# Moving the loads of gates and places of the experts to another queue and into seven blocks

## Chip, cores and metric

The kernel runs on one core of a Trainium2 chip. The metric is the device time of one launch in microseconds (us); lower is better.

## What is computed

A linear attention feeds a mixture of eight experts. The attention takes q, k and v of 8 batches, 8 heads, 576 rows and 64 columns; its output is seen as 4608 tokens of 512 values. Every token is routed to its two best experts.

```python
def _attn_ref(q, k, v):
    phi = lambda x: np.where(x > 0, x, np.exp(x) - 1.0) + 1.0
    q_p, k_p = phi(q), phi(k)
    kv = np.einsum('bhsd,bhse->bhde', k_p, v)
    num = np.einsum('bhsd,bhde->bhse', q_p, kv)
    den = np.einsum('bhsd,bhd->bhs', q_p, np.sum(k_p, axis=2))[..., None] + 1e-06
    return num / den

    # experts, x is 4608 x 512, w1 is 8 x 512 x 1024, w2 is 8 x 1024 x 512
    noisy_logits = x @ w_gate + np.log1p(np.exp(x @ w_noise)) * noise
    top2 = np.argpartition(-noisy_logits, 2, axis=1)[:, :2]
    # top2_w: the two gates of a token, a softmax over its two logits
    for e in range(E):
        for k in range(2):
            mask = top2[:, k] == e
            h = np.maximum(x[mask] @ w1[e], 0.0)
            out[mask] += top2_w[mask, k, None] * (h @ w2[e])
```

## The kernel before

The first part of the kernel computes attention and routing, and it scatters every token's row twice into a table in DRAM, `x_sorted` (`dispatch`, line 396, GpSimd): once into the list of first visits ("F") of the lower numbered of its two experts, once into the list of second visits ("S") of the other. A row of this table is 1152 bytes: the 512 values, and behind them four words, which are the token's number, its two gates, and its place in the list of first visits. A tile is 128 rows of such a list.

The second part works the experts through, block by block; a block is up to four tiles of one expert. `mm1` (line 652) makes the hidden layer of a block in eight pieces, and ScalarE takes each out of PSUM with a Relu (line 654). `mm2` (line 667) makes the output of one tile. VectorE multiplies it with the gate (lines 671 to 675), and where the tile is one of second visits, it adds the first visits' results `L`. `put` stores first visits into the DRAM table `part` by SyncE's queue (line 683) and scatters second visits to the output by GpSimd (line 689). `gather` (line 635, GpSimd) fetches `L` for the next block from `part`. It may start only when all first visits of the experts of lower number are stored. Tiles called "M" hold the end of both lists of an expert and are fetched by `mid_gather` (line 505, GpSimd); they count as both. GpSimd puts a MEMSET as a gap behind each of its indirect DMAs.

The order on every engine is the order of the program. `interval` (line 699) weaves the `mm1` of block i with the `mm2` and the `put` of block i-1, and ends with the `gather` for block i+1. In the main loop there are 20 blocks: block 0 is the last of expert 0 (called c0, tiles F6 to F9, the last a half tile), 1 and 2 belong to expert 1, 3 and 4 to expert 2, 5 to 7 to expert 3, and so on to 17 to 19 of expert 7. Each half of the weights of the experts 4 to 7 is loaded by GpSimd's queue (line 443) at the start of one of the blocks 1, 3, 4, 6, 8, 9, 11 and 12.

The gates and places of the lists are brought to SBUF by `meta_load` (line 450), as 16 bytes out of each row. For the first tiles of the experts 0 to 3 this is done early, in rounds, by SyncE's queue. The rest goes by GpSimd's queue: `prepare(0)`, called in `routing`, makes one load, and `prepare(1)` to `prepare(7)`, called all together in block 0, make 13, two for each of the experts 1 to 6 (F and S) and one of ten tiles for expert 7. In the queue of GpSimd they stand behind the last dispatch and ahead of two `mid_gather`s and of the first weights of expert 4. `metas(e)`, called in the last block before expert e, makes indices out of the lists on VectorE: `meta_s` out of the loaded list (lines 464 to 467) and `mid_meta` out of the M rows (lines 518 to 522). On VectorE they stand ahead of the outputs of the block before.

Of the kernel before, what the change touches and what calls it, by code (L numbers as in the profile page):

```python
# [15 lines left out]
P = 128  # L16
# [3 lines left out]
E = 8  # L20
# [392 lines left out]
class PhaseB:  # L413
# [31 lines left out]
    def meta_load(self, e, kind, i0, nt, group=None):  # L445

        m = self.mp.tile([P, nt, 4], INT32, name=f"meta{e}{kind}{i0}", bufs=1)
        row = self.row(e, kind, i0)
        rows = self.x_sorted[row : row + nt * P, HD // 2 : HD // 2 + 4]
        r = (self.nc.gpsimd if group is None else self.nc.sync).dma_start(out=m[:], in_=rows.rearrange("(t p) c -> p t c", p=P))  # L450
        self.early(r, kind, group)
        for i in range(nt):
            self.m[e, kind, i0 + i] = {"gate": m[:, i, 1 : 2] if kind == "F" else m[:, i, 2 : 3]}
        if kind == "S":
            self.raw[e] = m
# [456 lines left out]
def routing(pa, pb, c, a0, a1, a2):  # L912

    b0, b1 = pb.block(0, ("F", 4, 2)), pb.block(1, ("F", 3, 2))
    b2 = pb.block(2, ("F", 2, 2))
    a3, c0 = pb.block(3, ("F", 0, 3)), pb.block(0, ("F", 6, 4))
    pb.w_tiles(2, 1)
    pb.w_load(2, 0)
    pa.dispatch(2, 5, 6)
    pb.w_load(2, 1)  # L920
    pa.dispatch(2, 6, 9)
    pb.w_tiles(3, 1)
    pb.meta_load(0, "F", 4, 2, 2)
    pb.x_load(b0, 2)
    pb.meta_load(1, "F", 3, 2, 2)
    pb.x_load(b1, 2)
    pa.rt_b(3)
    pa.rt_c(3)
    pb.mm2(a0, 0)
    pb.put(a0, 0)  # L930
    pa.dispatch(3, 0, 6, (0,))
    pb.w_load(3, 0)
    pb.mm2(a0, 1)
    pb.put(a0, 1)
    pa.rt_a(4)
    pb.mm1(a1, *range(6))
    pa.rt_b(4)
    pb.mm1(a1, 6, 7)
    pa.rt_c(4)
    pa.dispatch(4, visits=(0,))  # L940
    pb.w_load(3, 1)
    pa.dispatch(3, 0, 6, (1,))
    pa.dispatch(4, visits=(1,))
    pb.mids()
    pb.meta_load(2, "F", 2, 2, 2)
    pb.x_load(b2, 2, False)
    pb.meta_load(3, "F", 0, 3, 2)
    pb.x_load(a3, 2, False)
    pb.interval(a2, a1, (), b0)
    pb.interval(b0, a2, (), b1)  # L950
    pb.prepare(0)
    pb.x_load(c0, turned=False)
    pb.interval(b1, b0, (), b2)
    pb.interval(b2, b1, (), a3)
    pb.interval(a3, b2, (), c0)
    return a3, c0
# [14 lines left out]

WEIGHTS = [(1, 3), (4, 6), (8, 9), (11, 12)]
TURNED = 3
AT = 0


@with_exitstack
def kernel(
    ctx: ExitStack,
    tc: tile.TileContext,  # L980
    q: bass.AP,
    k: bass.AP,
    v: bass.AP,
    moe_w_gate: bass.AP,
    moe_w_noise: bass.AP,
    moe_noise: bass.AP,
    moe_w1: bass.AP,
    moe_w2: bass.AP,
    out: bass.AP,
):  # L990
    nc = tc.nc
    x_sorted = nc.dram_tensor("x_sorted", (NO_X + 2 * P, ROW_W // 2), INT32, kind="Internal").ap()
    part = nc.dram_tensor("part", (NO_P + 2 * P, HD), FP32, kind="Internal").ap()
    nc.scalar.preload_act_table_set(ACT_SET)

    consts = ctx.enter_context(tc.tile_pool(name="consts", bufs=1))
    zrow = consts.tile([P, ROW_W // 2], INT32, name="zrow")
    pb = PhaseB(ctx, tc, moe_w1, moe_w2, x_sorted, part, out)
    pb.cp = consts
    ps = lambda cx, name, bufs, side: cx.enter_context(tc.tile_pool(name=name, bufs=bufs, space=PSUM, side=side))  # L1000
    ps_b = ps(ctx, "ps_b", 2, "left")
    pb.ps_h = pb.ps_y = [ps_b]
    with ExitStack() as order:
        order.enter_context(tc.manual_schedule())
        right = lambda name, bufs: ctx.enter_context(tc.tile_pool(name=name, bufs=bufs, side="right"))
        with ExitStack() as rout:
            ps_misc = ps(rout, "ps_misc", 2, "left")
            with ExitStack() as attn:
                psa = [ps(attn, "ps_num", 1, "right"), [(ps_misc, "misc"), (ps_b, "b")]]
                pa = PhaseA(attn, rout, tc, q, k, v, x_sorted, psa)  # L1010
                for t in "kqv":
                    pa.load(0, t)
                c = pa.c = pb.c = build_constants(tc, consts, moe_w_gate, moe_w_noise, moe_noise)
                pa.buffers()
                for t in "kv":
                    pa.load(1, t)
                first = attention(pa, pb, c, x_sorted, zrow)
            pb.ps_h = [ps(ctx, "ps_h2", 3, "right")]
            pb.ps_t = ps(ctx, "ps_t", 1, "right")
            pb.xps += [pb.xp] * 3 + [right("B_x2", 1)]  # L1020
            pb.np = right("B_n", 3)
            pb.lp = right("B_l", 8)
            pb.yp += [right("B_y2", 6)] * 2
            pb.wp.append(right("B_w2", 3))
            prev, cur = routing(pa, pb, c, *first)
        pb.ps_y.append(ps(ctx, "ps_y2", 2, "left"))
        pb.wp.append(ctx.enter_context(tc.tile_pool(name="B_w3", bufs=1, side="left")))
        pb.late = ctx.enter_context(tc.tile_pool(name="B_late", bufs=1, side="left"))
        blocks = [cur] + [pb.block(e, *parts) for e in range(1, E) for parts in PLAN[e]]

        todo = {}
        for e, at in zip(range(4, E), WEIGHTS):
            for k, i in enumerate(at):
                todo.setdefault(i, []).append((e, k))
        for i, b in enumerate(blocks):
            pb.left += [b["e"]] * sum(kind != "S" for kind, _ in b["tiles"])
        for i, b in enumerate(blocks):
            if i == AT:
                for e in range(1, E):
                    pb.prepare(e)  # L1040
            nxt = blocks[i + 1] if i + 1 < len(blocks) else None
            for nb in blocks[i + 1 : i + 4] if i == 0 else blocks[i + 3 : i + 4]:
                pb.x_load(nb, turned=nb["e"] >= TURNED)
            if (i == 0 or b["e"] != blocks[i - 1]["e"]) and b["e"] + 1 < E - 1:
                pb.mid_gather(b["e"] + 1)
            if nxt and nxt["e"] != b["e"]:
                pb.metas(nxt["e"])

            parts = todo.get(i, [])
            for e2, k in parts:  # L1050
                if k == 0:
                    pb.w_tiles(e2, {4: 1, 5: 2}.get(e2, 0))
            pb.interval(b, prev, parts, nxt)
            prev = b
        pb.interval(None, prev)
    pb.general()
# [30 lines left out]
```

## Time and profile before

| | us |
|---|---|
| median of three runs | 424.74 |
| lowest and highest | 424.2 and 425.75 |
| the profiled execution | 428.73 |
| its span | 426.9 |

In the profile, PE is TensorE, PEld its weight loads, DVE VectorE, ACT ScalarE, POOL GpSimd and SP SyncE. Over the span PE is busy 82%, POOL 68%, DVE 43% and ACT 41%. Each such share mixes the two parts of the kernel; the rows further down are of the second part, and they have the time in us from the start of the span. A row of a timeline has the start, the duration, the engine, the line, the operation, what is written from what, and in brackets how long the engine sat idle before and what ended that. Durations of DMA instructions are those of the issue; when the data has landed shows in who waits for it.

### The profile page before, as it was taken

Reading aid. Unit: us, or ns where it says so; the run is one execution under the profiler, and the core shown is the slowest. Engines: PE = TensorE matmul, PEld = TensorE weight load, DVE = VectorE, ACT = ScalarE, POOL = GpSimd, SP = SyncE. Lnnn points to the kernel's source line nnn. Section 1 sums busy time; section 2 is a strip of 40 time slices with the busy share of each in tenths; the row PEclk is TensorE's granted clock in tenths of the full one; section 3 lists DMA queues with packets and bytes.
Section 4 is the critical chain, followed back from the end, with each engine's and each line's share of the span. In section 5 each row is a group of like instructions: output and inputs, shape, how many; then the busy total and the mean of one; then the engine's idle time right before and its main releaser. Section 6 shows DMA issues by size and latency. Waiting matters only on the chain.

```text
span 426.9 us, 6907 instructions
## 1 busy us (share of the span) xinstructions
PE 348.1 (82%) x2517; PEld 206.5 (48%) x2517; DVE 184.2 (43%) x474; ACT 173.4 (41%) x310; POOL 289.3 (68%) x422
## 2 busy tenths in 40 slices
PE   3863577453757888999999999999999999999930
PEld 1363466353545454655556556545545544554410
DVE  2837989995777741111342305223322222412220
ACT  1738654760442432455445434443343343344200
POOL 7120229886888878737707675878848868989880
PEclk9987655688698998999999999999999999999985
DMA  9999999498998999994496999999998999944440
GB/s 128 205 208 208 236 208 229 105 227 198 214 191 204 204 219 227 254 364 105 87 252 191 171 189 250 211 245 253 187 284 174 226 280 232 212 157 154 140 165 25
DMA packets 77025, 85.58 MB, mean 200 GB/s; under 512 B 36415, under 2 KB 59730, under 8 KB 76982
## 3 DMA queue, kind: packets, MB, share of 16 engines
q0 software_dynamic: 36624, 64.02, 70.1%
q1 hardware_dynamic: 38694, 20.86, 21.9%
q10 hardware_dynamic: 1664, 0.18, 0.5%
q8 instruction: 21, 0.34, 0.3%
q14 instruction: 22, 0.18, 0.1%
HBM read 77.13 MB, written 33.79 MB: 260 GB/s over the span
## 4 chain that ended last, share of the span: by engine, by line
PE 41%; POOL 25%; DMA 18%; DVE 6%; issue 5%; ACT 2%; POOLq 0%; DVEq 0%; ACTq 0%
PE b L652 20%; PE b L667 19%; DMA w<-in_moe_w_dram 6%; POOL x_sorted L396 6%; POOL L L635 5%; POOL out_dram L689 5%; DMA kq<-in_q_dram 5%; DMA L<-part,mgi 2%; POOL gap L642 2%; POOL gap L697 2%; DMA xt<-x_sorted 2%; POOL gap L387 1%; DMA part<-y 1%; POOL kq L161 1%; PE t L599 1%
## 5 line engine op out<-in xcount | busy, mean ns | idle before, releaser
L654 ACT ACTIVATE hT<-b 128x256 bf16<-128x256 f32 (+5 forms) x224 | 101.7, 461 | 151.1 <-PE b L652 148.1
L652 PE MATMUL b<-xt,w 128*128 128x256 bf16 (+5 forms) x896 | 149.1, 314 | 15.4 <-DMA xt<-x_sorted 13.4
L667 PE MATMUL b<-w,hT 128*128 128x512 bf16 (+1 forms) x640 | 146.1, 384 | 0.0
L652 PEld LDWEIGHTS <-w 128*128 128x128 bf16 x896 | 86.5, 99 | 70.8 <-issue 20.3
L396 POOL DMA_INDIRECT x_sorted<-xr,posi x72 | 75.0, 1041 | 32.3 <-DMA w<-in_moe_w_dram 12.5
L667 PEld LDWEIGHTS <-hT 128*128 128x128 bf16 (+1 forms) x640 | 59.5, 100 | 64.6 <-issue 5.0
L176 ACT ACTIVATE e<-kq 128x2304 bf16<-128x2304 bf16 x16 | 33.2, 2120 | 24.8 <-PE misc L207 10.3
L635 POOL DMA_INDIRECT L<-part,gi x34 | 34.9, 1026 | 6.1 <-issue 6.1
L689 POOL DMA_INDIRECT out_dram<-y,si x34 | 33.7, 992 | 6.1 <-issue 5.3
L635 POOL DMA_INDIRECT L<-part,mgi x12 | 12.0, 1001 | 32.0 <-DMA xt<-x_sorted 15.4
L207 PE MATMUL b<-v,e 64*128 64x192 bf16 x144 | 19.3, 309 | 11.2 <-DVE e L188 8.7
L671 DVE SCALAR_TENSOR_TENSOR y<-b,mgate,L 128x512 f32<-128x512 f32 (+1 forms) x12 | 8.9, 745 | 42.7 <-DMA L<-part,mgi 24.6
L270 PE MATMUL num<-kvbd,pqt 128*64 128x162 bf16 x288 | 18.3, 299 | 11.0 <-DVE lwt L288 10.1
L281 DVE TENSOR_TENSOR xr<-num,rden 128x768 bf16<-128x768 f32 x24 | 21.9, 953 | 4.8 <-DMA x_sorted<-xr,posi 4.5
L207 PEld LDWEIGHTS <-e 64*128 64x128 bf16 x288 | 17.0, 122 | 14.2 <-DVE e L188 9.4
L270 PEld LDWEIGHTS <-pqt 128*64 128x64 bf16 x288 | 15.3, 146 | 13.6 <-DVE lwt L288 8.1
L188 DVE TENSOR_TENSOR e<-e,kq 128x2304 bf16<-128x2304 bf16 x16 | 21.5, 1358 | 0.3
L642 POOL MEMSET gap<- 128x416 f32 x46 | 21.2, 460 | 0.1
L697 POOL MEMSET gap<- 128x416 f32 x45 | 21.0, 466 | 0.0
L207 PE MATMUL misc<-v,e 64*128 64x192 bf16 x144 | 19.5, 309 | 0.6 <-DMA v<-in_v_dram 0.6
L387 POOL MEMSET gap<- 128x192 f32 x72 | 19.8, 275 | 0.0
L256 ACT COPY pqt<-misc 128x1024 bf16<-128x1024 bf16 (+1 forms) x15 | 13.6, 905 | 14.9 <-PE misc L254 14.7
(184 smaller groups left out, 327.8 us busy)
## 6 DMA issues: line engine op xcount, KB each, us to landing
w<-in_moe_w_dram POOLq DMA_DIRECT2D x16, 1024.0 KB
part<-y SPq DMA_DIRECT2D x39, 256.0 KB, 5.5
kq<-in_k_dram POOLq DMA_DIRECT2D x8, 576.0 KB
kq<-in_q_dram POOLq DMA_DIRECT2D x8, 576.0 KB
v<-in_v_dram POOLq DMA_DIRECT2D x8, 576.0 KB
x_sorted<-xr,posi POOLq DMA_INDIRECT x72
xn<-x_sorted SPq DMA_DIRECT2D x4, 256.0 KB, 6.8
part<-y SPq DMA_DIRECT2D x7, 128.0 KB, 6.9
```

The source lines that it names most:

```text
L176: self.nc.scalar.activation(out=e, in_=x, func=ACT.Exp)
L207: nc.tensor.matmul(out=self.kvps[g, h, j][:, KVM * i : KVM * i + KVM], lhsT=e[half, hp, ci, :], rhs=v[half, hp::4, 64 * ci : 64 * ci + 64] ...
L270: nc.tensor.matmul(out=ps[half, hp, KVW * i : KVW * i + KVW], lhsT=self.pqt[g, 3 * t + i][:, hp, half], rhs=self.kvbd[g][:, j, hp, :], sta ...
L387: self.nc.gpsimd.memset(self.c["gap"], 0.0)
L396: r = self.nc.gpsimd.indirect_dma_start(out=self.x_sorted, out_offset=bass.IndirectOffsetOnAxis(ap=self.r["posi", u][:, ci - c0, sl : sl + ...
L635: r = nc.gpsimd.indirect_dma_start(out=L[0:m].bitcast(INT32), out_offset=None, in_=self.part.bitcast(INT32), in_offset=bass.IndirectOffset ...
L642: nc.gpsimd.memset(self.c["gap2"][:], 0.0)
L652: nc.tensor.matmul(out=ps[:, 0:n], lhsT=w1[:, dc, fc * P : fc * P + P], rhs=b["xt"][:, dc, 0:n], start=(dc == 0), stop=(dc == 3))
L654: nc.scalar.activation(out=b["hT"][:, fc, 0:n], in_=ps[:, 0:n], func=ACT.Relu)
L667: nc.tensor.matmul(out=ps[i * m : i * m + m], lhsT=b["hT"][:, f, t * P : t * P + m], rhs=w2[:, f, :], start=(fc == 0), stop=(fc == 8 // n ...
L689: r = nc.gpsimd.indirect_dma_start(out=self.out, out_offset=bass.IndirectOffsetOnAxis(ap=self.m[e, kind, i]["si"][0:m], axis=0), in_=y[0:m ...
L697: nc.gpsimd.memset(self.c["gap2"][:], 0.0)
```

## The change

The 13 loads of the experts 1 to 7 go by ScalarE's queue instead of GpSimd's, and those of expert e are issued at the start of block e-1, so in the blocks 0 to 6. The test on `e` also sends the remaining load of expert 0 by SyncE's queue.

```diff
@@ meta_load
-        r = (self.nc.gpsimd if group is None else self.nc.sync).dma_start(out=m[:], in_=rows.rearrange("(t p) c -> p t c", p=P))
+        r = (self.nc.scalar if e and group is None else self.nc.sync).dma_start(out=m[:], in_=rows.rearrange("(t p) c -> p t c", p=P))
@@
-AT = 0
@@ main loop
         for i, b in enumerate(blocks):
-            if i == AT:
-                for e in range(1, E):
-                    pb.prepare(e)
+            if i < E - 1:
+                pb.prepare(i + 1)
```

## Rows read from the trace of the kernel before

**Rows 1.** The page's chain that ended last: shares of the span by engine.

```profile
PE 41%; POOL 25%; DMA 18%; DVE 6%; issue 5%; ACT 2%; POOLq 0%; DVEq 0%; ACTq 0%
```

**Rows 2.** That chain in order of time: start, us, what; its last 82 us.

```profile
345.10 5.40 DMA part<-y
351.33 1.05 POOL L L635
...
380.71 1.05 POOL L L635
...
414.88 0.97 POOL out_dram L689
```

**Rows 3.** Stretches of 5 us: busy of PE, PEld, DVE, ACT, POOL; PEclk; DMA share; GB/s.

```profile
200.00:205.00 5.00, 5.00 (x32) 2.62 (x31) 0.00 (x0) 2.98 (x5) 4.70 (x6) 1.00 0.29 12
...
220.00:225.00 5.00, 5.00 (x36) 2.99 (x34) 2.21 (x9) 1.46 (x3) 0.00 (x0) 1.00 1.18 289
```

**Rows 4.** GpSimd's timeline, from the loads of the lists to the gather for expert 2.

```profile
194.51 0.57 POOL L450 DMA_DIRECT2D meta1S<-x_sorted  x1 [3.98 <-DMA x_sorted<-xr,posi]
...
202.63 1.09 POOL L450 DMA_DIRECT2D meta7S<-x_sorted  x1
204.02 1.07 POOL L505 DMA_INDIRECT xm<-x_sorted,m_idx  x1 [0.30 <-issue]
...
210.41 0.83 POOL L443 DMA_DIRECT2D w<-in_moe_w_dram  x1
226.62 1.06 POOL L635 DMA_INDIRECT L<-part,mgi  x1 [15.37 <-DMA xt<-x_sorted]
...
234.54 0.98 POOL L443 DMA_DIRECT2D w<-in_moe_w_dram  x1
...
243.42 1.04 POOL L635 DMA_INDIRECT L<-part,mgi  x1 [2.88 <-issue]
```

**Rows 5.** VectorE's timeline: the indices of expert 1, and outputs of several experts.

```profile
197.99 0.16 DVE L466 TENSOR_TENSOR si<-meta1S,inv 128x1 int32<-128x1 int32 x1 [4.59 <-DMA meta1S<-x_sorted]
...
209.17 0.16 DVE L518 TENSOR_TENSOR mgate<-xm 128x2 f32<-128x2 f32 x1 [10.95 <-DMA xm<-x_sorted,m_idx]
...
219.02 0.75 DVE L675 SCALAR_TENSOR_TENSOR y<-b,meta0F,y 64x512 f32<-64x512 f32 x1
...
234.10 0.74 DVE L671 SCALAR_TENSOR_TENSOR y<-b,mgate,L 64x512 f32<-64x512 f32 x1 [1.56 <-PE b L667]
...
255.77 0.75 DVE L671 SCALAR_TENSOR_TENSOR y<-b,mgate,L 128x512 f32<-128x512 f32 x1 [12.79 <-DMA L<-part,mgi]
...
308.22 0.74 DVE L671 SCALAR_TENSOR_TENSOR y<-b,mgate,L 64x512 f32<-64x512 f32 x1 [3.30 <-issue]
...
408.96 0.75 DVE L671 SCALAR_TENSOR_TENSOR y<-b,meta7S,L 128x512 f32<-128x512 f32 x1 [0.97 <-PE b L667]
```

**Rows 6.** TensorE's timeline: one full output tile, and two half tiles.

```profile
197.44 1.89 PE L667 MATMUL b<-w,hT 128*128 128x512 bf16 x8
...
233.00 1.05 PE L667 MATMUL b<-w,hT 128*64 128x512 bf16 x8
...
304.18 1.05 PE L667 MATMUL b<-w,hT 128*64 128x512 bf16 x8
```

**Rows 7.** SyncE's timeline: the last store of first visits.

```profile
373.88 0.48 SPq L683 DMA_DIRECT2D part<-y  x1
```

**Rows 8.** Min/median/max: landing of stores to part (us); issues of lines 450, 573 (ns).

```profile
DMA to landing us min/median/max: 3.6/6.1/10.6
...
L450 SPq DMA_DIRECT2D meta3F<-x_sorted x1: 645/645/645, 164.5 to 164.5; - x1
...
L573 SPq DMA_TRANSPOSE xt<-x_sorted x23: 1227/1654/5762, 105.5 to 357.6; - x23
```

**Rows 9.** ScalarE's timeline around the start of the blocks 0 and 1.

```profile
196.12 0.49 ACT L654 ACTIVATE hT<-b 128x384 bf16<-128x384 f32 x1 [0.15 <-PE b L652]
...
210.84 0.82 ACT L654 ACTIVATE hT<-b 128x256 bf16<-128x256 f32 x2 [1.78 <-PE b L652]
```

## The prediction

> **What bounds the kernel now.** I read the chain of waits first, by shares: it runs 41% through TensorE, 25% through GpSimd, 18% through DMA [rows 1]. Then the chain in order of time. Up to about 320 us it is TensorE's own work, piece after piece; from there it follows GpSimd, with an occasional landing of a store between, and ends on GpSimd's last scatter at 414.88 [rows 2]. The stretches of the same time show TensorE busy 5.00 of 5 us at a granted clock of 1.00, that is at the upper of its two levels [rows 3], and the 43 stretches from 190 to 405 us, of which two stand here, all read so. TensorE is thus never late in this part, and nothing can make it earlier. Its last output is ready for the scatter when VectorE ends it, at 408.96 + 0.75 = 409.71 [rows 5], but GpSimd scatters it at 414.88 [rows 2]. GpSimd trails TensorE by 5.2 us at the end: all that any change to GpSimd, VectorE or the loads can win here, and no more.
>
> Third, GpSimd's own timeline, for where the lists stand in it. Of the 13 loads of the experts 1 to 7, the first of second visits waits until 194.51 for the dispatch to land, and the last, of ten tiles, begins at 202.63 and takes 1.09 us. Behind them stand the first fetch of M rows at 204.02 and the first weights of expert 4 at 210.41; then GpSimd sits idle for 15.37 us, until 226.62 [rows 4]. The trace names a transposing load as what ended it. The program says that this gather waits for the last store of expert 0, whose output VectorE ends at 219.02 + 0.75 = 219.77 [rows 5]. I take that store: 6.85 us from the output to its landing fits the median landing of 6.1 [rows 8].
>
> Last, VectorE, the waits by engine: 4.59 us for the list of expert 1 and 10.95 us for the M rows behind it in GpSimd's queue [rows 5]. Outputs of TensorE wait behind both until after 209.17, in PSUM, without holding TensorE up.
>
> **The change, part by part.** *Off GpSimd.* From 194.51 to the fetch at 204.02 are 9.5 us. The fetch needs the same dispatch to have landed, so it can start at 194.5, no sooner, and the weights of expert 4 come at 210.41 - 9.5 = 200.9. VectorE gets its M rows some 8 to 9 us earlier. Neither is late for anyone now: GpSimd's idle 15.37 us swallow the 9.5 whole, and VectorE's next output of expert 0 is bound by TensorE. Directly this part is worth 0.
>
> *What moves with it.* The weights now cross the memory around 201 to 212 us instead of around 211 to 224. At 200 to 205 the DMA engines are at 0.29 of their time; at 220 to 225, with these weights in them, at 1.18 [rows 3]. The last store of expert 0 goes out in that second stretch. Without the weights it should land like the quickest store, 3.6 us, not in 6.85 less its issue [rows 8]. Bounds: 0 (the store lands as before) to 6.85 - 3.6 = 3.2 us. I take 2.6, nearer the quick end, because the largest transfer of the stretch is gone. So the gather moves from 226.62 to about 224.0, and with it, back to back in GpSimd's queue, the second half of these weights, from 234.54 to about 231.9 [rows 4].
>
> *Whether it is carried on.* At 234.10 VectorE is bound by TensorE again (half tile from 233.00 for 1.05 [rows 6]), so the store of expert 1 doesn't move, and the gather of expert 2 at 243.42 [rows 4] may gain little. But its rows land only at 255.77, 12.3 us later [rows 5], and they stand in the same queue behind the weights of 234.54, which now end 2.6 us earlier. I expect them 2 to 2.6 us earlier. From there the loop is the same for each expert: gather, its landing, the last output of the expert, its store, the landing (345.10, 5.40 us), the next gather (351.33) [rows 2]. Each step waits for the one before, so a lead is handed on, until TensorE or a store sets a floor. Two floors are near. For expert 4 TensorE ends the half tile at 304.18 + 1.05 = 305.23 and VectorE starts on it at 308.22: a lead of up to 3.0 us passes [rows 5, 6]. For expert 7 the gather at 380.71 [rows 2] needs the store of 373.88 [rows 7], which lands no sooner than 373.9 + 0.5 + 3.6 = 378.0: 2.7 us pass [rows 7, 8]. From 351.33 GpSimd works without a pause, so what is left of the lead at 380.71 is the gain at the end. Of 2.6 I keep 2.2, since five landings lie between and the first may hand on less.
>
> *Onto ScalarE.* 13 issues in the blocks 0 to 6, two at each start, one for the last. The nearest row is SyncE's issue of a list of three tiles, 0.645 us; the far bound is SyncE's longest issue of any kind, 5.76 us [rows 8]. I take 0.6 to 1.2 us by number of tiles, 1.3 us at a start on average. The work that hides it: ScalarE's next Relu waits for TensorE 1.78 us at the start of block 1 [rows 9]; beyond that TensorE has three PSUM buffers, and after two pieces it does a full output tile, 1.89 us [rows 6], before it needs the first buffer again. Cover about 1.8 + 1.7 = 3.5 us, cost 0. In block 0, which ScalarE comes to when its Relu ends at 196.12 + 0.49 = 196.61 [rows 9], I count on the 1.7 us alone, still over 1.3. What its loads wait for, the dispatch, has landed by 194.5, 2.1 us before. Then VectorE has expert 1's list at about 196.6 + 1.3 + 3 = 201, where 3 is the 198.0 - 195.1 that it took from GpSimd's issue [rows 4, 5], and no longer waits until 209.17.
>
> *Onto SyncE.* One issue, by the same row 0.65 us, ahead of the rows of block 0, which TensorE takes only a block later: 0. Its wait for the dispatch of first visits is the one that the load behind it has anyway.
>
> *Later transfers.* The lists of the experts 2 to 7 now land between 210 and 262 us, where the DMA engines are busy. In 200 to 205, with hardly anything else running, they took 0.29 of the engines' time [rows 3]; over the 9 us of all loads that is 2.6 us, so some 0.4 us for an expert. Bounds for the end: 0 to +2.6. I take 0; each list has a block or more before it is read.
>
> **Sum.** 428.73 - 2.2 for the profiled execution; the runs have a median of 424.74, 0.93% below it, so I forecast 424.74 - 2.2 = 422.5.
>
> **The rivals.** *B, swallowed.* The store of expert 0 lands as before, or its lead is lost at 243.42, where the store of expert 1 sets the gather whatever GpSimd did. For it: DMA stays busy there, and VectorE is at TensorE's floor at 234.10. Against it: the 12.3 us of landing behind the weights. Time 424.7. The Trainium skill, "DMA: Bandwidth & Descriptors", section "Issuing engines are not separate DMA queues", speaks for B: loads started by different engines share the same 16 DMA engines, and starting them elsewhere saves only the issuing time. By that rule 9.5 us of GpSimd's time are all that is saved, the idle 15.37 us take them, and the time stays at 424.7.
>
> *C, ScalarE is held.* An issue on a busy queue takes far longer than 0.65 us. It decides from 3.5 us a start: above it Relu comes too late, PSUM fills and TensorE, which has no reserve, stops. At 5.76 us in each of the blocks 3 to 6 that is 4 x 2.3 = 9 us, of which the lag of GpSimd hides some 3 to 4: 424.7 + 5 = 430. For it: DMA is crowded there. Against it: the lists that SyncE loads took 0.65 us at most.
>
> *D, collisions.* The lists land among gathers and weights and stretch some of the five landings, up to +2.6, against or with the lead: 424 to 427.
>
> **How the numbers follow.** A (lead carried) has 0.54, of which 0.44 is over 0.5% and 0.10 under; its own range is 421.5 to 423.6. B has 0.25, all within 0.5%. C has 0.10, slower. D has 0.11: 0.06 within, 0.05 slower. Half a percent, 2.1 us, is about what a measurement of this kernel can tell from no change. That gives 0.44, 0.41 and 0.15. The range of 8 in 10 takes in all of A with its floors and B, and D up to its bound with the runs' scatter: 421.0 to 426.5; it leaves out C.
>
> **What would show it.** Right: the weights of expert 4 issued near 201, VectorE's M rows near 201, the gather near 224, the gather at 351.33 and the last scatter each 2 to 2.6 us earlier, TensorE still at 5.00 of 5. B: the same up to 224, but 243.42 and 351.33 where they were. C: pauses of TensorE at the starts of blocks, with ScalarE late. D: longer landings of gathers between 235 and 270. I would be wrong altogether if VectorE's wait at 198 stayed as long, because the list of expert 1 lands late, or if GpSimd's order of scatters at the end changed.

## The result, and the profile after

The median of 20 runs is 421.72 us, against 425.18 for 20 runs of the kernel before in the same session. The ratio is 0.989, with a 95% interval of 0.9865 to 0.9915: 4.7 us less, between 3.6 and 5.7. Ratios here leave out the runs that are over 1.5% above their kernel's fastest, 3 of the 20 before and 5 of the 20 after; the two medians, of all runs, are 3.5 us apart. The prediction had 2.2 us less; on the 424.74 from which it starts the ratio makes 420.1, below its range. The profiled execution took 420.32 us, its span 418.5 us.

The two profiled spans differ by 8.4 us, more than the runs do. Cut at four points that both traces have, the difference is in two pieces, and only one of them can be tied to the change:

| stretch | before, us | after, us | difference |
|---|---|---|---|
| start to TensorE's first 448-column piece of block 0 | 199.16 | 195.10 | 4.06 |
| from there to the end of VectorE's last output | 210.55 | 210.43 | 0.12 |
| from there to GpSimd's last scatter | 5.17 | 4.74 | 0.43 |
| from that scatter to the end of the span | 12.02 | 8.23 | 3.79 |

The rows on which these cuts rest, the first of the kernel before, the others of the kernel after (the other ends are in [rows 2] and [rows 5], and below):

```profile
199.16 1.68 PE L652 MATMUL b<-xt,w 128*128 128x448 bf16 x8
195.10 1.68 PE L652 MATMUL b<-xt,w 128*128 128x448 bf16 x8
404.78 0.75 DVE L671 SCALAR_TENSOR_TENSOR y<-b,meta7S,L 128x512 f32<-128x512 f32 x1 [0.98 <-PE b L667]
```

The first stretch is code that the change hardly touches, and it scatters: the next eight executions, of both kernels and of variants, have it between 195.9 and 198.1 (the changed kernel's second at 195.9, the other's at 198.0), the ten after them between 194.1 and 208.5. Whether the change has a small part in it isn't shown. Below, "from block 0" means a time counted from this first piece, which takes this scatter out. The last stretch is where the gain is. I had not looked at it.

It isn't in the chain of waits, which ends on the last scatter in both kernels; the rest of the span stands only in rows of line 738, the test ahead of a path that isn't taken, and of the line whose block is the whole program (1082 before, 1080 after). Here are those rows of both kernels: line, engine, operation, count, then min/median/max in ns, and the first and last start in us. First the kernel before:

```profile
L738 POOLq INC_SWDGE_SEM  x1: 1740/1740/1740, 417.9 to 417.9; - x1
L1082 POOLq DRAIN  x3: 46/103/6357, 419.7 to 426.6; - x3
```

And the kernel after:

```profile
L738 POOLq INC_SWDGE_SEM  x1: 1040/1040/1040, 413.1 to 413.1; - x1
L1080 POOLq DRAIN  x3: 46/103/3498, 414.2 to 418.3; - x3
```

Some 3 us after the last scatter, presumably when it has landed, GpSimd's sequencer runs an instruction INC_SWDGE_SEM (in `general`, the path for overfull lists, which is passed by here), and at the program's end a DRAIN. Together they took 8.10 us before and 4.54 after: 3.56 of the 3.79 us.

The steps of the prediction can be read in GpSimd's timeline after [rows 4]:

```profile
191.55 1.05 POOL L505 DMA_INDIRECT xm<-x_sorted,m_idx  x1 [5.52 <-DMA x_sorted<-xr,posi]
...
198.51 0.85 POOL L443 DMA_DIRECT2D w<-in_moe_w_dram  x1
219.07 1.04 POOL L635 DMA_INDIRECT L<-part,mgi  x1 [19.72 <-issue]
...
326.64 0.99 POOL L443 DMA_DIRECT2D w<-in_moe_w_dram  x1
...
344.26 0.92 POOL L689 DMA_INDIRECT out_dram<-y,msi  x1 [3.50 <-DMA w<-in_moe_w_dram]
345.81 1.05 POOL L635 DMA_INDIRECT L<-part,mgi  x1 [0.16 <-issue]
...
354.95 1.04 POOL L635 DMA_INDIRECT L<-part,gi  x1 [1.08 <-issue]
...
410.27 0.97 POOL L689 DMA_INDIRECT out_dram<-y,si  x1 [0.17 <-issue]
```

The 13 loads are gone from between the dispatch and the fetch of M rows; the weights come at 198.51, and the idle time behind them is now 19.72 us.

On VectorE [rows 5] the M rows of expert 1 come 1.1 us behind its list, where it was 11.2:

```profile
195.63 0.16 DVE L466 TENSOR_TENSOR si<-meta1S,inv 128x1 int32<-128x1 int32 x1 [6.30 <-DMA meta1S<-x_sorted]
...
196.76 0.16 DVE L518 TENSOR_TENSOR mgate<-xm 128x2 f32<-128x2 f32 x1 [0.90 <-DMA xm<-x_sorted,m_idx]
```

The issues on ScalarE's queue, of 13 the shortest, the longest and the last (the columns are those of the rows of the end above):

```profile
L450 ACTq DMA_DIRECT2D meta1S<-x_sorted x1: 334/334/334, 193.1 to 193.1; - x1
...
L450 ACTq DMA_DIRECT2D meta2S<-x_sorted x1: 720/720/720, 204.2 to 204.2; - x1
...
L450 ACTq DMA_DIRECT2D meta7S<-x_sorted x1: 374/374/374, 250.4 to 250.4; - x1
```

And TensorE, which did not notice, in the two stretches of [rows 3], with the same columns:

```profile
200.00:205.00 5.00, 5.00 (x30) 2.75 (x29) 0.75 (x1) 2.08 (x5) 0.00 (x0) 1.00 0.91 173
220.00:225.00 5.00, 5.00 (x39) 3.36 (x37) 0.65 (x1) 3.16 (x7) 4.51 (x8) 1.00 0.74 176
```

The weights have moved into the first of them: its DMA share is 0.91 where it was 0.29, and the second is at 0.74 where it was 1.18.

### The profile page after: what moved, and what is told of

Read it like the earlier page. It is cut to its first block, busy times and chain, and to the rows that moved or that the text cites. A ratio compares the mean times of both kernels' runs of the same rounds, so it can differ in the third digit from the quotient of the medians.

```text
span 418.5 us, 6918 instructions
## 1 busy us (share of the span) xinstructions
PE 343.8 (82%) x2517; PEld 204.2 (49%) x2517; DVE 184.4 (44%) x474; ACT 172.7 (41%) x310; POOL 278.7 (67%) x408
## 4 chain that ended last, share of the span: by engine, by line
PE 55%; POOL 20%; DMA 10%; DVE 6%; issue 4%; ACT 3%; POOLq 0%; DVEq 0%; ACTq 0%
PE b L667 26%; PE b L652 26%; POOL x_sorted L396 8%; DMA v<-in_v_dram 4%; POOL out_dram L689 4%; DMA w<-in_moe_w_dram 3%; POOL L L635 2%; DMA xt<-x_sorted 2%; POOL gap L387 2%; POOL gap L697 2%; DVE e L188 1%; PE b L207 1%; PE t L599 1%; POOL gap L642 1%; POOL kq L161 1%
## 5 line engine op out<-in xcount | busy, mean ns | idle before, releaser
L207 PE MATMUL b<-v,e 64*128 64x192 bf16 x144 | 19.5, 311 | 12.6 <-DVE e L188 10.0
L270 PE MATMUL num<-kvbd,pqt 128*64 128x162 bf16 x288 | 16.3, 277 | 11.0 <-DVE lwt L288 10.3
L270 PEld LDWEIGHTS <-pqt 128*64 128x64 bf16 x288 | 13.6, 134 | 13.6 <-DVE lwt L288 7.9
L256 ACT COPY pqt<-misc 128x1024 bf16<-128x1024 bf16 (+1 forms) x15 | 13.6, 905 | 16.0 <-PE misc L254 15.6
## 6 DMA issues: line engine op xcount, KB each, us to landing
kq<-in_q_dram POOLq DMA_DIRECT2D x8, 576.0 KB, 14.1
```

The lines of the kernel that those rows point to most:

```text
L207: nc.tensor.matmul(out=self.kvps[g, h, j][:, KVM * i : KVM * i + KVM], lhsT=e[half, hp, ci, :], rhs=v[half, hp::4, 64 * ci : 64 * ci + 64] ...
L270: nc.tensor.matmul(out=ps[half, hp, KVW * i : KVW * i + KVW], lhsT=self.pqt[g, 3 * t + i][:, hp, half], rhs=self.kvbd[g][:, j, hp, :], sta ...
```

## The experiments

**Both kernels once more.**

> The kernel before, once more, for a second profile. Of the 8.4 us between the two profiled spans (426.9 to 418.5), 4.1 lie ahead of block 0, in code that the change does not touch, 0.5 in GpSimd's lag behind TensorE at the end, and 3.8 behind the last scatter. Theory chance: TensorE's start of block 0 and the stretch behind the last scatter (12.0 us before, 8.2 after) both scatter by several us from execution to execution, so this profile may show either. Theory tail: the stretch behind the last scatter belongs to the kernel; here it is again 12.0 within 0.5, and GpSimd's last DRAIN takes 6.4 us again.

> The changed kernel, once more, for a second profile. Theory tail: behind the last scatter 8.2 us within 0.5, GpSimd's last DRAIN 3.5 us. Theory chance: anything from 8 to 12 us. Theory lead (the prediction): the last scatter trails TensorE's last output by 2.5 to 3 us less than before's 5.2; the first profile of after showed 4.7, which speaks against it.

The kernel before took 426.95 us (span 425.2), the changed one 420.51 (span 418.6). What repeats to the nanosecond is the end: 1740 and 6357 ns before, 1040 and 3498 ns after, with 12.05 and 8.23 us from the last scatter to the end. The lag of the last scatter behind VectorE's last output is 4.15 us before and 4.05 after. So in two executions of each the lag was 5.17 and 4.15, and 4.74 and 4.05: the lead on which the prediction rested shortens the lag by about 0.3 us, which is within its scatter.

**One half of the change alone.** The lists stay on GpSimd's queue, but are spread over the blocks:

```diff
-            if i == AT:
-                for e in range(1, E):
-                    pb.prepare(e)
+            if i < E - 1:
+                pb.prepare(i + 1)
```

> Loads stay on GpSimd's queue, but one expert's goes out in each of the blocks 0 to 6. GpSimd issues as many loads as before. Theory lead: the first weights of expert 4 still come 6 us earlier, so most of the gain, 2 us or 0.5%, is here. Theory tail (the number of loads on GpSimd makes the end longer): the stretch behind the last scatter is 12 us as before, and the time is within 0.5% of before or slower, since four loads now stand ahead of scatters in the later blocks.

Ratio 1.0073 (1.0026 to 1.0119), but the medians of all runs go the other way, 428.39 us for 429.27 before. It is no gain; whether it costs anything is open. In its one profile, with a span of 424.7 us, the end was that of before (1740 and 6357 ns, 12.03 us), and only the lag was longer, 5.53 us.

The other half: ScalarE's queue, but all 13 in block 0.

```diff
-        r = (self.nc.gpsimd if group is None else self.nc.sync).dma_start(...)
+        r = (self.nc.scalar if e and group is None else self.nc.sync).dma_start(...)
```

> All 13 loads go by ScalarE's queue, but together at the start of block 0. Theory tail: GpSimd issues 14 loads less, as in after, so the stretch behind the last scatter is 8.2 us and the time some 3.6 us (0.85%) below before, whatever the blocks do. Theory lead: GpSimd is as early as in after, so the gain is that of after too, unless 13 issues of 0.6 us in a row (8 us) hold the Relus and TensorE, which has cover for some 2 to 3.5 us: then 4 to 5 us of TensorE's time are lost and the time is equal to before or above.

Ratio 1.0164 (1.0099 to 1.0229). The end was that of after (1040 and 3498 ns, 8.43 us), but the stretch from block 0 to the last output took 223.1 us in place of 210.5. The issues on ScalarE's queue show why; two of the 13 in a row stall:

```profile
L450 ACTq DMA_DIRECT2D meta5S<-x_sorted x1: 729/729/729, 200.4 to 200.4; - x1
L450 ACTq DMA_DIRECT2D meta6F<-x_sorted x1: 4980/4980/4980, 201.2 to 201.2; - x1
L450 ACTq DMA_DIRECT2D meta6S<-x_sorted x1: 459/459/459, 206.2 to 206.2; - x1
L450 ACTq DMA_DIRECT2D meta7S<-x_sorted x1: 2331/2331/2331, 206.7 to 206.7; - x1
```

Its waits by engine (what waited, for what: us in total, times, longest) show ScalarE's Relu behind them, and TensorE behind the Relu:

```profile
ACT hT L654 <- DMA meta6S<-x_sorted: 13.5, 1, 13.5
PE b L652 <- ACT hT L654: 10.7, 1, 10.7
```

That is rival C, at a price of 12.7 us, where all 13 loads stand together. Two at a time, as in the change, cost TensorE nothing. Of the 12.7 us, TensorE's wait is 10.66; most of the rest is its clock. After it had stood still since about 199 us, the granted clock was at 0.50, the lower of its two levels, and the first output tile took 3.02 us where it takes 1.89 (TensorE's timeline, then the stretches with the columns of [rows 3]):

```profile
209.72 1.65 PE L652 MATMUL b<-xt,w 128*128 128x448 bf16 x4 [10.66 <-ACT hT L654]
211.17 3.02 PE L667 MATMUL b<-w,hT 128*128 128x512 bf16 x8
```

```profile
208.00:211.00 3.00, 1.27 (x4) 0.54 (x4) 0.00 (x0) 1.42 (x3) 0.00 (x0) 0.50 0.68 25
214.00:217.00 3.00, 3.00 (x22) 1.72 (x21) 0.75 (x1) 2.00 (x3) 0.00 (x0) 1.00 0.23 87
```

So the place alone brings no gain, and the queue alone costs more than it brings: the queue brings the shorter end, the place makes it affordable.

**Is it ScalarE's queue?** The changed kernel, with all lists on SyncE's:

```diff
-        r = (self.nc.scalar if e and group is None else self.nc.sync).dma_start(...)
+        r = self.nc.sync.dma_start(...)
```

> One expert's lists in each of the blocks 0 to 6, as in after, but by SyncE's queue. GpSimd issues 216 loads as in after. Theory tail: the end is 8.2 us and the time that of after, some 0.9 to 1.1% below before, and ScalarE's queue has no part in the gain. Theory ScalarE (its queue lands lists earlier or relieves SyncE's stores): the end is 8.2 us, but SyncE's stores come later and the time is 0.5% or more above after.

Ratio 0.9877 (0.9832 to 0.9922), the same gain as the change within the intervals. The end was 1040 and 3498 ns again, 8.71 us. For the end, what counts is what comes off GpSimd's queue, not where it goes.

**The path for overfull lists left out.** INC_SWDGE_SEM stands in it; this kernel is the one before without its call `pb.general()`.

> The kernel before without the general path for overfull lists (the branch that is not taken with this draw, and the load of its condition); lists and all other work as before, 230 loads on GpSimd. Theory tail: the long end is the price of passing that branch by, since GpSimd makes up for its loads there, so without it the stretch behind the last scatter is 3 to 5 us, 7 to 9 less than before's 12.0. Theory drain: the last DRAIN waits for GpSimd's loads themselves and stays at 6.4 us, the stretch at 9 us or more.

One execution: 422.91 us, span 421.1, 8.17 us from the last scatter, a figure that neither theory had. INC_SWDGE_SEM is gone, but not the DRAIN:

```profile
L1081 POOLq DRAIN  x3: 51/97/8462, 411.8 to 420.8; - x3
```

The sequencer comes to it while the last scatters are still under way. So the DRAIN belongs to the program's end, whatever the path. Without the path the end of the kernel before is 3.9 us shorter, about as much as the change takes off it.

**Does it go with the number of GpSimd's loads?** The changed kernel with 8 and with 14 further loads of two tiles of list each on GpSimd's queue, which nobody reads:

```diff
         for e, i in weights:
             self.w_load(e, i)
+        for j in range(self.idle_loads):
+            t = self.mp.tile([P, 2, 4], INT32, name=f"idle{j}", bufs=1)
+            rows = self.x_sorted[self.row(1, "F", 0) : self.row(1, "F", 2), HD // 2 : HD // 2 + 4]
+            r = self.nc.gpsimd.dma_start(out=t[:], in_=rows.rearrange("(t p) c -> p t c", p=P))
+            self.early(r, "F", None)
@@ main loop
+            pb.idle_loads = 14 if i == 1 else 0
```

> The same with 8 loads. Theory count: 8/14 of the way, a stretch of 8.2 + 2.2 = 10.4 us, DRAIN 3.50 + 1.63 = 5.13 us, the instruction ahead of it 1.44. Theory turn (GpSimd's loads go by eight semaphores in turn, and it matters only where in the turn the last one stands: 216 loads in after are 27 whole turns, 230 before leave 6 over): 8 more are a whole turn, so 8.2, 3.50 and 1.04 us as in after.

> The changed kernel with 14 more loads on GpSimd's queue, which nobody reads, in the stretch of block 1 where it sat idle for 19.7 us; everything else as in after. Theory count (the end behind the last scatter grows with the number of loads that GpSimd has issued): the stretch is 12.0 us as before (8.2 in after), GpSimd's last DRAIN 6.36 us and the instruction ahead of it 1.74, so the time is 3.8 us above after's, 0.1 to 0.3% below before's. Theory lists (it is what is loaded and read that makes the end long): 8.2, 3.50 and 1.04 us, and the time of after.

Ratios to the kernel before 0.9886 (0.9819 to 0.9953) and 0.995 (0.9915 to 0.9985). With 14 loads the end is

```profile
L744 POOLq INC_SWDGE_SEM  x1: 1460/1460/1460, 413.5 to 413.5; - x1
L1087 POOLq DRAIN  x3: 46/103/5213, 415.0 to 420.8; - x3
```

and 10.54 us in all; with 8 it is 1320 and 4642 ns, 9.82 us. As many loads as the lists had give back 2.3 of the 3.8 us, so it isn't the count of loads. Nor is it the place of the last load in a turn of eight, since eight more loads, a whole turn, add 1.6 us. The number of pieces (the contiguous runs that a load is made of) orders the kernels: 14 loads of two tiles are 224 pieces for each of the 16 DMA engines (14 x 2 x 128 / 16), the lists of the kernel before, 50 tiles, are 400. (The queues bear out the 50 tiles: with the change those of ScalarE and SyncE have 6096 and 528 packets more, 50 x 128 and 16 for each of 14 loads. Two expectations below count one more for each load and put the lists at 382 for each engine; it is 414.)

**Does it grow with all that GpSimd describes?** The same kernel, with idle loads of 9, 13 or 16 pieces of 8 bytes for each partition.

```diff
+            t = self.mp.tile([P, 9, 2], INT32, name=f"idle{j}", bufs=1)
+            rows = self.x_sorted[self.row(1, "F", 0) : self.row(1, "F", 1), 0 : 72].rearrange("p (t c) -> p t c", c=8)
+            r = self.nc.gpsimd.dma_start(out=t[:], in_=rows[:, :, 0:2])
```

> After with 10 idle loads on GpSimd of 128 x 9 short pieces each, in the same stretch. So far the last DRAIN has stood at 3.498, 4.642, 5.213 and 6.357 us (0, 2, 3 and 5 steps of 0.572), and the pieces added on GpSimd, counted for each of the 16 DMA engines as pieces/16 plus one for a load, at 0, 136, 238 and 382: some 76 for a step. Here 730. Theory amount (the end grows with all that GpSimd has described): 9 to 10 steps, DRAIN 8.6 to 9.2 us, the stretch behind the last scatter 15 to 16 us. Theory ring (GpSimd fills a ring, and only its place in the ring at the end counts): less as soon as the ring has come round, DRAIN anywhere between 0 and 9 us, and on a lower branch of a saw for one of the four kernels at least.

> As the kernel before it in this series, 14 loads, 1022 added for each DMA engine. Theory amount: 13 steps, DRAIN 10.9 to 11.5 us. Theory ring: a step count that lies below that, by the length of the ring; with a ring of 1024 it is after's 3.5 us again.

> 12 loads of 128 x 13, 1260 added for each DMA engine. Theory amount: 16 to 17 steps, DRAIN 12.6 to 13.2 us. Theory ring: lower; with a ring of 1024 it is 3 steps above after, 5.2 us.

> 14 loads of 128 x 16, 1806 added for each DMA engine; they no longer fit in GpSimd's idle stretch, so the blocks behind may run late, and only the end counts. Theory amount: 23 to 24 steps, DRAIN 16.6 to 17.2 us. Theory ring: lower; with a ring of 1024 it is 10 steps above after, 9.2 us.

The largest of these loads did not make the largest end. With ten of nine pieces a partition, 720 for each engine, it was the shortest so far:

```profile
L744 POOLq INC_SWDGE_SEM  x1: 520/520/520, 416.3 to 416.3; - x1
L1087 POOLq DRAIN  x3: 46/103/1375, 416.9 to 418.8; - x3
```

So it does not grow with all that is described. It rises, falls, rises again at 14 loads of nine, and falls again behind them; but the figures that I had written down for a ring of 1024 were missed as well. (With 12 loads of 13, and 14 of 16, the longer spans come from the blocks, 221.1 and 216.9 us from block 0 to the last output, not from the end.)

**One curve for both kernels?** If the end follows the amount, up to a point at which it starts anew, then the kernel before must climb on with a few such loads, and fall at the point where the changed one falls. I had put that point too early.

> The kernel before (all lists by GpSimd, all in the first block), with one load more on GpSimd's queue in the interval of block 1: 128 x 9 pieces of 8 bytes that nobody reads, about 73 descriptors for each DMA engine. The runs so far fit one count n in each kernel: INC_SWDGE_SEM takes 20 ns x n and the DRAIN 81.7 ns x n - 750 ns, with n = 87 before, 52 after, 66 and 73 with 8 and 14 small idle loads, 26 with 10 loads of 128 x 9. Theory ring: n is the number of GpSimd's last DMAs that it has issued since its descriptors last filled a ring of about 1000 for each DMA engine, and what is described earlier moves that point. One load of 73 moves it to 6 to 9 DMAs earlier: n = 93 to 96, INC 1.86 to 1.92 us, DRAIN 6.85 to 7.10, 12.6 to 13.0 us from the last scatter to the end. Rival lists: the cost belongs to the lists on GpSimd's queue, however many pieces stand beside them: 1.74 and 6.36 as before, 12.0 us.

> The kernel before with two such loads. Theory ring: 146 descriptors more lie at the edge at which the ring fills once more: n is either about 101 to 105 (INC 2.0 to 2.1 us, DRAIN 7.5 to 7.8, 13.5 us behind the last scatter) or, if it is just past it, under 6 (INC under 0.12 us, hardly a DRAIN, about 3.6 us). Rival lists: 1.74 and 6.36, 12.0 us.

> The kernel before with three such loads: GpSimd describes more than in any version timed so far that has all lists on its queue. Theory ring: the ring has filled once more shortly before the end, n = 7 to 12, INC 0.14 to 0.24 us, DRAIN 0.05 to 0.25, about 3.8 us from the last scatter to the end in place of 12.0; the three loads themselves hold GpSimd's DMAs up by some 0.5 us, so the kernel before gains 7.5 us of 425 by work added: ratio 0.982. Rival lists: 12.0 us behind the last scatter and 0.5 us for the loads: ratio 1.001. Rival amount (cost grows with all that is described): over 13 us, ratio 1.004.

> The changed kernel with eight such loads in the interval of block 1. Theory ring: 584 descriptors more, n = 6 to 11, about 3.8 us from the last scatter to the end in place of 8.2; the loads cost some 1.2 us of GpSimd's lead (10 of them: lag of the last scatter 5.3 us where it was about 3.8): ratio 0.981 to 0.984 to the kernel before, where the change alone has 0.989. The rivals (lists, amount): 8.2 us or more, and 1.2 us lost: ratio 0.992.

The first two came close to what the ring theory had, 12.55 and 13.60 us from the last scatter, where the theory that the lists themselves cost wanted 12.0. The third and fourth did not fall, as the ring theory wanted; they rose, as the theory of the amount had it: 14.14 us and a ratio of 1.005 (0.9993 to 1.0107) with three loads on the kernel before; a ratio of 1.0011 (0.9962 to 1.0059) with eight on the changed one, whose end is

```profile
L744 POOLq INC_SWDGE_SEM  x1: 2020/2020/2020, 425.8 to 425.8; - x1
L1087 POOLq DRAIN  x3: 46/103/7500, 427.9 to 436.0; - x3
```

Eight such loads thus give the changed kernel an end of 9.5 us by these two instructions, and ten gave 1.9. That is either the point, or the ten were an accident:

> The changed kernel with ten idle loads of 128 x 9 pieces, as once before, now timed. Theory ring: GpSimd's count n behind the last scatter is again 26 (INC 0.52 us, DRAIN 1.375 us, 5.6 us to the end) although the kernel with two such loads fewer had 101 (2.02, 7.50, 13.4 us): the ring has filled once more in between. Ratio to the kernel before 0.985 to 0.990 (the end is 6.5 us shorter than before's, the loads take 1 to 1.5 us). If the short end was an accident of one execution, n is over 101 and the ratio about 1.002.

> The kernel before (all lists by GpSimd, all in the first block) with five such loads; one, two and three gave n = 92, 101 and 103 and ends of 12.5, 13.6 and 14.1 us, so a ring of 1000 was too small an estimate. Theory ring, with the size that the runs now allow (10 loads on the changed kernel, 730 descriptors for each engine, have passed it, 3 loads on the kernel before, 382 and 219, have not): 382 and 365 give 747, so the ring has filled once more: n = 15 to 35, INC 0.3 to 0.7 us, DRAIN 0.5 to 2.1, 4.5 to 6.5 us behind the last scatter in place of 12.0, and the kernel before becomes faster by work that nobody needs: ratio 0.984 to 0.990. Rival amount or lists: n = 103 or more, 14 us or more, ratio 1.005.

The ten repeat it to the nanosecond:

```profile
L744 POOLq INC_SWDGE_SEM  x1: 520/520/520, 413.8 to 413.8; - x1
L1087 POOLq DRAIN  x3: 46/103/1375, 414.4 to 416.3; - x3
```

Their ratio is 0.9835 (0.9796 to 0.9874), median 419.27 us, the fastest version here. It was timed in another session than the change, and the two intervals overlap from 0.9865 to 0.9874, so that it beats the change is likely rather than shown. Its lag, 4.42 us, is no longer than the change's (4.74 and 4.05).

Five of these loads on the kernel before, whose lists are all on GpSimd's queue, also pass the point:

```profile
L744 POOLq INC_SWDGE_SEM  x1: 940/940/940, 426.0 to 426.0; - x1
L1089 POOLq DRAIN  x3: 46/103/3090, 427.0 to 430.6; - x3
```

The end falls from 14.14 us with three loads to 7.78, by added work. The kernel as a whole did not gain, ratio 1.0148 (1.0104 to 1.0193): from block 0 to the last output it took 223.4 us in place of 210.5. The fetch of M rows for expert 4, issued at 247.5 and 249.2, landed late,

```profile
DMA to landing us min/median/max: 22.9/23.5/24.2
```

and TensorE stood waiting for it, 3.92 us at 271.72; it waited 3.68 us more for VectorE at 314.37. Behind both the granted clock was about half (0.54 in 273 to 276, 0.50 in 315 to 318), and an output tile took 3.57 us where it takes 1.89. In the changed kernel the landing of the fetch in that stretch is

```profile
DMA to landing us min/median/max: 8.6/8.6/8.6
```

Why it is late there is open. My expectation, that the whole kernel would gain, is refuted; the one about the end is borne out, though the two instructions came out longer than I had put them (0.94 and 3.09 us, not 0.3 to 0.7 and 0.5 to 2.1).

All the ends in one table, by pieces that GpSimd describes for each DMA engine beyond the changed kernel's:

| kernel | pieces beyond after's | INC_SWDGE_SEM, ns | DRAIN, ns | last scatter to end, us |
|---|---|---|---|---|
| after; queue alone; SyncE's queue | 0 | 1040 | 3498 | 8.2; 8.4; 8.7 |
| after + 8 loads of 2 | 128 | 1320 | 4642 | 9.8 |
| after + 14 loads of 2 | 224 | 1460 | 5213 | 10.5 |
| before; place alone | 400 | 1740 | 6357 | 12.0; 12.0 |
| before + 1 load of 9 | 472 | 1840 | 6765 | 12.6 |
| before + 2 of 9 | 544 | 2020 | 7500 | 13.6 |
| after + 8 of 9 | 576 | 2020 | 7500 | 13.4 |
| before + 3 of 9 | 616 | 2060 | 7663 | 14.1 |
| after + 10 of 9, twice | 720 | 520 | 1375 | 5.6; 5.6 |
| before + 5 of 9 | 760 | 940 | 3090 | 7.8 |
| after + 14 of 9 | 1008 | 1940 | 7173 | 13.8 |
| after + 12 of 13 | 1248 | 1260 | 4397 | 9.5 |
| after + 14 of 16 | 1792 | 760 | 2355 | 7.0 |

Kernels with the lists on GpSimd's queue and without them lie on one rising curve from 0 to 616 pieces. It has broken off at 720 in the changed kernel and at 760 in the kernel before, and rises again. Neither the loads nor the bytes order the rows: eight loads of 2 and eight of 9 end with 1320 and 2020 ns, and those eight of 9 bring 74 KB, the lists 102 KB with 1740 ns. The two instructions go together: in every row INC_SWDGE_SEM is a multiple of 20 ns, and the DRAIN is, within 3 ns, 3498 ns + 81.7 ns for each 20 ns by which INC_SWDGE_SEM exceeds 1040, or less by as much. Both thus seem to count the same thing, 87 of it before and 52 after. 400 pieces more are 35 more of it, so it isn't the pieces themselves.

The times follow the end. The change's 3.79 us alone make a ratio of 0.991, inside its interval. The measured 0.989 and the difference between a variant's end and the change's make 0.993 and 0.994 for 8 and 14 loads of 2, 1.001 for 8 of 9 and 0.983 for 10 of 9; measured were 0.9886, 0.995, 1.0011 and 0.9835. Three loads of 9 on the kernel before should make 1.005, and did.

## Why the prediction was wrong

*What bounds the kernel.* Right as far as the last scatter, wrong about the end. The failed step is the sentence that 5.2 us are "all that any change to GpSimd, VectorE or the loads can win here, and no more". Behind the scatter at 414.88 [rows 2] lay another 12.02 us of the span of 426.9, of which 8.10 were GpSimd's INC_SWDGE_SEM and DRAIN. I took the last row of the chain for the end of the program, and did not compare it with the span. This term, 3.8 us, is absent from the sum. From the trace of before alone its size could have been seen, but hardly that the change would shrink it.

*Off GpSimd, directly 0.* Right for the timeline: the idle 15.37 us took the 9.5 and became 19.72. Wrong for the time, because what GpSimd described there was paid for again at the end, with 3.8 us.

*What moves with it.* Right: the weights at 198.51 are, from block 0, at 3.4 where they were at 11.3, and the first gather at 24.0 in both profiles, where it was at 27.5 in the profile before and 25.9 in its repeat: a lead of 3.5 and 1.9 us, where 2.6 was forecast.

*Whether it is carried on.* The mis-sized term: 2.2 us predicted, 0.55 between the two first profiles, 0.71 between the two second. The starts of the gathers from block 0, of the first row for each expert:

| gather for expert | 1 | 2 | 4 | 5 | 6 | last scatter |
|---|---|---|---|---|---|---|
| before | 27.5 | 44.3 | 83.5 | 118.3 | 152.2 | 215.7 |
| after | 24.0 | 44.3 | 80.6 | 114.5 | 150.7 | 215.2 |
| before again | 25.9 | 44.2 | 82.5 | 116.0 | 151.7 | 215.2 |
| after again | 24.0 | 43.7 | 80.7 | 114.1 | 150.0 | 214.5 |

At expert 2 the lead is gone or 0.5 us, as rival B had it, and it is there again at the experts 4 and 5. In the first pair most of it is lost before expert 6. The scatter at 344.26 stands in GpSimd's queue ahead of that gather and waited 3.50 us for the last weights. (It is the eighth DMA behind them in that queue; why it waits for them isn't shown.) In the kernel before the same two instructions are

```profile
334.58 1.00 POOL L443 DMA_DIRECT2D w<-in_moe_w_dram  x1
...
348.43 0.92 POOL L689 DMA_INDIRECT out_dram<-y,msi  x1 [1.21 <-DMA w<-in_moe_w_dram]
```

The weights' issue comes at 135.4 from block 0 before and at 131.5 after, the scatter behind their landing at 149.3 and at 149.2. So the earlier issue won nothing, 17.6 us from it to the scatter for 13.9. This is a floor that I had not named beside my two. It is one of the first pair only: in the second the issues come at 134.1 and 131.1 and the scatters at 150.1 and 147.9, so most of the lead passes. In both pairs 1.5 to 1.7 us are left at expert 6, and another 0.9 us goes at a pause of 1.08 us that only the changed kernel has, ahead of 354.95. From there to the last scatter both kernels take 55.32 us.

*Onto ScalarE, 0.* Right. 13 issues of 334 to 720 ns, 5.78 us in all, all but two below the 0.6 to 1.2 us each that I had taken. Rival C's price stands in the kernel with all of them in one block, 12.7 us: all 13 in a row stall where two don't, which the prediction had not put as its condition; what exactly fills up isn't shown. One of my signs of being wrong altogether came too, without harm: VectorE's wait for the list of expert 1 did not shrink (6.30 us for 4.59), though the one behind it, for the M rows, fell from 10.95 to 0.90, and TensorE noticed neither.

*Onto SyncE, later transfers, 0.* Nothing in the runs speaks against the first. The second I can't separate from the late weights above.

*Rival B* came nearest in what it said of the lead. Its rule from the Trainium skill ("DMA: Bandwidth & Descriptors", section "Issuing engines are not separate DMA queues"), that starting loads elsewhere saves only the time of issuing, would give 424.7 us; by the runs the move also saved 3.8 us at the program's end, whichever queue took the loads.

*The sum, remade:* 3.8 us at the end and 0.55 to 0.71 of lead (the last scatter from block 0, in the two pairs of profiles) are 4.3 to 4.5, inside the measured 3.6 to 5.7. The 3.8 repeats; the lead doesn't stand out from the scatter, since the lag alone ran from 2.1 to 6.4 us over all the kernels here.

## What to carry to other kernels

Compare the last row of the chain with the span before saying what can be won; what lies between has rows too, of the engines' sequencers. Of a load taken off GpSimd's queue, count the pieces it names and not only its time in the queue, and read the last INC_SWDGE_SEM and DRAIN of both kernels; that part can also rise when work is taken away. A lead in one queue can be lost at anything that stands later in that queue and waits for a landing, so follow it to the end, in more than one profile. And a stall of TensorE can cost more than its own length, by the clock behind it.

## What the runs showed of the hardware

The end of a program that loads through GpSimd has a price that repeats to the nanosecond, between 1.9 us (520 and 1375 ns) and 9.7 us (2060 and 7663 ns) here, and goes up and down with the number of pieces that GpSimd's loads have, useful or idle. A reading that fits the rise and the break is a store of descriptors which is emptied when it is full, and an end that clears step by step, by 20 ns and again by 82, what has come since. The Trainium skill ("DMA: Bandwidth & Descriptors", section "SWDGE vs HWDGE vs iDMA") says that GpSimd writes its descriptors to rings in SBUF; the trace agrees so far as the end goes up and down with what GpSimd describes, and not with what ScalarE or SyncE issue. No run shows the ring itself, nor its size, and the sizes that the expectations took were missed: on the common curve the break lies between 616 and 720 pieces beyond the changed kernel's, and the second rise is steeper than the first (520, 940 and 1940 ns at 720, 760 and 1008 pieces). What exactly is counted stays open.

ScalarE's queue took ten issues in a row at 335 to 729 ns; the eleventh took 4980 ns. And TensorE, when it had stood still for 10.66 us behind them, went on at a granted clock of 0.50, which was 1.00 again by 214 to 217 us.
